# Attention and soft mixture of experts on one core: loads paced from another place in each 256 TensorE instructions, key block 3 asked for sooner, and another order of work in the last stage

## The chip, the cores and the metric

The kernel runs on one core of one Trainium2 chip. The metric is the device time of one execution in microseconds (us). Three runs of the kernel before gave a median of 335.19 us (332.28 to 336.5). The profiled execution is one further run.

## The reference

Attention over 8 batches, 8 heads, 512 local and 32 global tokens of width 64, then a soft mixture of 8 experts with 4 slots each, over the 4,608 tokens of width 512 that the attention gives. All inputs and the output are float32.

```python
s_g  = scale * q_g @ [k_g, k_l]^T              # global queries see every key
s_ll = where(|pos_i - pos_j| <= 32, scale * q_l @ k_l^T, -1e9)
s_l  = [scale * q_l @ k_g^T, s_ll]             # local queries: global keys and a window
out  = softmax(s) @ [v_g, v_l]                 # softmax with + 1e-9 in the denominator
x    = out as (4608, 512)                      # tokens x (heads * 64)
logits = x @ phi                               # 4608 x 32 slots
d = softmax over the tokens;  slot_in = d.T @ x            # 32 x 512
slot_out[e] = relu(slot_in[e] @ w1[e]) @ w2[e]             # 8 experts, 4 slots each
c = softmax over the slots;   return c @ slot_out          # 4608 x 512
```

## The kernel before

The order of the work on every engine is written out by hand: each engine executes its instructions in the order in which the Python code names them, and semaphores hold back one that needs another engine's result.

**Attention** takes 32 steps, one for two heads of one batch (four steps a batch). Step s issues the four copies of values on GpSimd (POOL) that `make_v` makes, the global queries' products on TensorE (PE) when s is even, the scores of step s+1 (`scores`, tile pS), their maximum and shift on VectorE (DVE), the transposes into pT, the values product of step s-1 (128 matmuls in tile pO) and the exponentials on ScalarE (ACT). Once a batch it adds logits and the running slot inputs (`sums`, `add_sums`). A step has some 350 to 460 PE instructions. A float32 matmul is two passes, each a weight load and a matmul, so `mm` counts it as 4.

**Loads.** All transfers are issued by SyncE (SP), from one list, `queue`: "k" is a block of keys and queries for a step (tile kq, 624 KB, 3 buffers), "v" its values (390 KB, 5 buffers), "p" a page of expert weights that stays resident (tile w, 512 KB), "b" a page in a buffer that attention is done with. `counted` adds up the PE instructions. When the count has passed a multiple of 256 by at least 8, it calls `pump`, which issues loads from the list as long as their sum is under BUDGET (with `debt` carried to the next call) and makes each of them wait for the PE instruction at which it was called. `need` issues without such a wait what a step cannot go without: before, `need(kqs, 3)` at the head of step 2 is where key block 3 is issued, behind the list's earlier entries.

**The last stage** follows the last batch's sums. `turn_logits` transposes the logits. `first_product(r, ph)` multiplies the slot inputs of experts 4r to 4r+3 by w1; `denominators` inside it has the DVE wait for a small PE product. `hidden` is relu and scale on the DVE, 8 transposes into pM on PE and two copies on ACT. `weights(g)` is the softmax over slots (DVE, ACT, DVE), `turn_weights(g)` its transpose into pT and a copy on ACT. `second_product(h, m0, m1)` multiplies by the half h of w2's columns, `slot_outputs` brings the sum into tile sa, and `combine(h, b)` multiplies the combine weights of batch b by sa, copies the result out of pS, pT or pM (ACT and DVE in turn) and stores 512 KB (tile ob). Weight pages 47 to 54 (`new_slot`, i from 0) go into the buffers of w1 pages that the first product has read, and so do pages 55 to 63.

Of the kernel before, what the change touches and what calls it, by code (L numbers as in the profile page):

```python
# [7 lines left out]
F32 = mybir.dt.float32  # L8
# [6 lines left out]
B, H, SL, SG, D = 8, 8, 512, 32, 64  # L15
E, SE, DM, FF = 8, 4, 512, 1024
NS = E * SE
P = 128
VD = D + 1
NP = 4 * B  # L20
# [22 lines left out]
NBF = 192 + 512  # L43

NRES = 30


def block_window(c):
# [11 lines left out]
def kernel(ctx, tc, kq, vS, phi, w1, w2, cst, cbf, out):  # L60
# [13 lines left out]
    pS = psum.tile([P, 2, 512], F32, name="pS")  # L74
    pT = psum.tile([P, 2, 512], F32, name="pT")
    pO = psum.tile([P, 2, 512], F32, name="pO")
    pM = psum.tile([P, 2, 512], F32, name="pM")
    pM0, pM1 = pM[:, 0, :], pM[:, 1, :]
# [19 lines left out]
    def bc(ap, n):  # L98
        return ap.unsqueeze(len(ap.shape)).broadcast_to(list(ap.shape) + [n])
# [4 lines left out]


    npe = [0]
    block = [0]

    def counted(n, ins):
        npe[0] += n  # L110
        if npe[0] // 256 > block[0] and npe[0] % 256 >= 8:
            block[0] = npe[0] // 256
            pump(ins)
        return ins

    def mm(o, l, r, start=True, stop=True):
        return counted(2 if l.dtype == BF16 else 4, nc.tensor.matmul(o, l, r, start=start, stop=stop))  # L117

    def tr(o, src, idn):
        return counted(2, nc.tensor.transpose(o, src, idn))  # L120
# [15 lines left out]
    queue, wt = [], {}  # L136
    npage = [0]
# [4 lines left out]
    def page_into(t):  # L142
        k, e, a, f = pages[npage[0]]
        npage[0] += 1
        wt[k, e, a, f] = t
        return nc.sync.dma_start(t, w1[e, a] if k == 0 else w2[e, a, f])
# [9 lines left out]
    def in_slot(i, shape, dtype, name):  # L156
        return slots[i].tile(shape, dtype, tag=f"pg{i}", name=name, bufs=1)
# [5 lines left out]
    def load_borrowed(_):  # L163
        pool, tag = (kqp, "kq") if len(slots) < NRES + 3 else (wp, "w")
        slots.append(None)
        return page_into(pool.tile([P, 1024], F32, tag=tag, name=f"w{npage[0]}"))

    LOAD = {"b": (load_borrowed, 512 * 1024), "k": (load_kq, 128 * KQC * 4), "v": (load_v, 128 * 6 * 2 * VD * 4), "p": (load_res, 512 * 1024)}

    queue = [("k", 0), ("k", 1), ("v", 0), ("k", 2), ("v", 1), ("v", 2), ("p", 0), ("v", 3), ("p", 0), ("v", 4), ("p", 0)]  # L170
    for s in range(3, NP, 2):
        queue += [("k", s)] + ([("k", s + 1)] if s + 1 < NP else []) + [("p", 0)]
        queue += [("v", v) for v in (s, s + 1) if 5 <= v < NP]
        queue += [("p", 0)]
    np_left = NRES - sum(k == "p" for k, _ in queue)
    assert np_left <= 0, np_left
# [5 lines left out]
    def allowed(kind, s):  # L182
        if kind == "k":
            o = s - 3
            return o < 0 or now["a"] >= (o if o % 2 == 0 else o - 1)
        if kind == "v":
            o = s - 5
            return o < 0 or now["c"] >= 2 * (o // 2) + 2
        return now[s[0]] >= s[1] if kind == "b" else True

    BUDGET = 1_150_000
    debt = [0]

    def issue(after=None):
        kind, s = queue.pop(0)
        f, size = LOAD[kind]
        ins = f(s)
        if after is not None:
            tc.add_manual_dep(ins.ins, after.ins.name, mybir.DependencyInfo(
                mybir.DependencyClass.Sync, mybir.DependencyReason.DATA), reason="pace")  # L200
        return size

    def pump(after):
        got = debt[0]
        while queue and allowed(*queue[0]) and got + LOAD[queue[0][0]][1] / 2 < BUDGET:
            got += issue(after)
        debt[0] = max(0, got - BUDGET)

# [394 lines left out]
    two_pages()  # L603


    hTs = {}

    def denominators():
        tot = pT[:, 1, 1:2]
        mm(tot, qmat, wl)  # L610
        nc.vector.tensor_scalar_add(rt, tot, GUARD)
        nc.vector.reciprocal(rt, rt)
        nc.vector.tensor_scalar_mul(rte, con[:, C_EM:C_EM + 2], rt)

    def first_product(r, ph):
        for hc in range(4):
            if hc == 3 and r == 0:
                denominators()
            for n in range(2):
                for j in range(4):  # L620
                    mm(ph[32 * j:32 * j + 32, n, :], sT[hc // 2][:, hc % 2, :],
                       wt[0, 4 * r + j, hc, 0][:, 512 * n:512 * n + 512], hc == 0, hc == 3)

    def hidden(r, ph):
        hs = in_slot(8 + r, [P, 2, 512], F32, f"hs{r}")
        hTs[r] = in_slot(10 + r, [P, 8, P], F32, f"hT{r}")
        for n in range(2):
            nc.vector.tensor_scalar(hs[:, n, :], ph[:, n, :], 0.0, rte[:, r:r + 1], ALU.max, ALU.mult)
        for n in range(2):
            for f in range(4):  # L630
                tr(pM[:, n, P * f:P * f + P], hs[:, n, P * f:P * f + P], ident)
            nc.scalar.copy(hTs[r][:, 4 * n:4 * n + 4, :], pM[:, n, :].rearrange("p (f q) -> p f q", f=4))
# [4 lines left out]
    def turn_logits(g, bank):  # L637
        for k in range(4):
            tr(bank[:, P * k:P * k + P], lT[:, 4 * g + k, 0:P], ident)

    def weights(g, bank):
        n = 16 if g < 2 else 2
        lvs[g] = xp.tile([P, n, NS], F32, tag="xT", name=f"lv{g}", bufs=4) if g < 2 else keep.tile([P, n, NS], F32, name="lvg")
        lv, cm = lvs[g], xp.tile([P, 16], F32, tag="cm", name=f"cm{g}")
        c = cm[:, 0:n]
        if g < 2:
            v = bank.rearrange("p (t s) -> p t s", s=NS)
        else:
            v = lv
            for k in range(2):  # L650
                nc.vector.transpose(lv[:, k, :], lT[:, (4, 7)[k], P:LW])
        nc.vector.reduce_max(c, v, axis=AX.X)
        nc.vector.tensor_tensor(lv, v, bc(c, NS), ALU.subtract)
        nc.scalar.activation(lv, lv, AF.Exp)
        nc.vector.reduce_sum(c, lv, axis=AX.X)
        nc.vector.tensor_scalar_add(c, c, GUARD)
        nc.vector.reciprocal(c, c)
        nc.vector.tensor_tensor(lv, lv, bc(c, NS), ALU.mult)

    def turn_weights(g, bank):  # L660
        lv = lvs[g]
        if g < 2:
            cTs[g] = xp.tile([P, 4, P], F32, tag="xT", name=f"cT{g}", bufs=4)
            for k in range(4):
                tr(bank[:, P * k:P * k + P], lv[:, 4 * k:4 * k + 4, :].rearrange("p t s -> p (t s)"), ident)
            nc.scalar.copy(cTs[g], bank.rearrange("p (k q) -> p k q", k=4))
        else:
            cTs[g] = keep.tile([2 * NS, 1, P], F32, name="cTg")
            tr(bank[0:2 * NS, 0:P], lv.rearrange("p t s -> p (t s)"), ident)
            nc.scalar.copy(cTs[g][:, 0, :], bank[0:2 * NS, 0:P])  # L670

    def second_product(h, m0, m1):
        for m in range(m0, m1):
            r, f = m // 8, m % 8
            for j in range(4):
                mm(pO[32 * j:32 * j + 32, h, 0:256], hTs[r][:, f, 32 * j:32 * j + 32],
                   wt[1, 4 * r + j, h, f // 4][:, 256 * (f % 4):256 * (f % 4) + 256], m == 0, m == 15)
# [3 lines left out]
    def slot_outputs(h):  # L681
        nc.vector.tensor_copy(so[:, h], pO[:, h, 0:256])
        mm(pO[:, h, 0:256], qmat, so[:, h])
        nc.vector.tensor_copy(sa[:, h], pO[:, h, 0:256])
# [6 lines left out]
    def combine(h, b):  # L691
# [11 lines left out]
        else:  # L703
            for gg in range(2):
                nc.sync.dma_start(ov[4 * gg:4 * gg + 4, 0:SG, cs], o[:, gg, :])

    turn_logits(0, pM0)
    turn_logits(1, pM1)
    first_product(0, pO)
    new_slot = lambda i: page_into(in_slot(i, [P, 1024], F32, f"w{npage[0]}"))  # L710
    for i in range(8):
        new_slot(i)
    weights(0, pM0)
    weights(1, pM1)
    weights(2, None)
    turn_weights(0, pT[:, 0, :])
    turn_weights(1, pT[:, 1, :])
    hidden(0, pO)
    turn_weights(2, pT[:, 0, :])
    first_product(1, pS)  # L720
    i = 16
    while npage[0] < len(pages):
        new_slot(i)
        i += 1
    assert i <= 26, i
    second_product(0, 0, 4)
    hidden(1, pS)
    second_product(0, 4, 16)
    so = keep.tile([P, 2, 256], F32, tag="xg0", name="so")
    sa = keep.tile([P, 2, 256], F32, tag="acc", name="sa")  # L730
    slot_outputs(0)
    for b in range(B + 1):
        combine(0, b)
    second_product(1, 0, 16)
    slot_outputs(1)
    for b in range(B + 1):
        combine(1, b)
# [74 lines left out]
```

## Time and profile before

| | |
|---|---|
| median of three runs | 335.19 us (332.28 to 336.5) |
| the profiled execution's own time | 336.67 us |
| its span, first to last instruction | 334.9 us |
| PE / DVE / ACT / POOL busy | 244.9 / 158.0 / 120.9 / 100.8 us |
| moved by DMA | 77.10 MB, mean 230 GB/s |
| mean granted TensorE clock | 0.908 of full speed |

The attention runs from the first scores at 6.5 us to about 241 us, the serial end of the slot softmax to about 257 us, then the expert products and the output to 334.9 us. Busy shares are means over these stages; what ends a stage is read from the waits in it. In the rows, "<-issue" is idle time in which the engine waited for no semaphore that the profile shows. "pO L117 x64" is a group of 64 matmuls made in line 117 (`mm`) with result in pO. Numbers after an instruction in square brackets are its idle time before it and who ended it.

### The profile page before, as it was taken

The numbers are of one execution on the slowest core, as the hardware profiler recorded it, in microseconds if no ns is written. First come the engines' busy times: TensorE is split into PE (matmuls) and PEld (weight loads), VectorE is DVE, ScalarE is ACT, GpSimd is POOL, SyncE is SP. The second block draws the span as 40 slices with busy tenths as digits, with TensorE's granted clock in tenths as the row PEclk, the third lists the DMA queues.
The fourth block names the chain that finished last, engine by engine and source line by source line (L and its number), as shares of the span: only waits on it lengthen the run. The fifth ranks groups of instructions, "written<-read, shape, count | busy, mean of one in ns | idle before, by whom it ended". The sixth has DMA issues, their size and how long they took to land.

```text
span 334.9 us, 15942 instructions
## 1 busy us (share of the span) xinstructions
PE 244.9 (73%) x7345; PEld 166.7 (50%) x7345; DVE 158.0 (47%) x269; ACT 120.9 (36%) x279; POOL 100.8 (30%) x196
## 2 busy tenths in 40 slices
PE   8629568678757978776867877788668739979850
PEld 5417457547535766562756466476433223445420
DVE  0733553728465485573627465674441370133340
ACT  0413443435444355552435345454630021123230
POOL 1630535253363543734243443724400000000000
PEclk9996987979999799996979989999987967999985
DMA  7774776855777773873864596751799852939594
GB/s 239 292 251 159 257 241 222 277 186 156 243 250 230 257 272 115 264 251 131 263 226 141 151 326 203 259 155 42 216 373 396 308 217 106 406 125 338 182 342 139
DMA packets 27907, 77.10 MB, mean 230 GB/s; under 512 B 2368, under 2 KB 11456, under 8 KB 27840
## 3 DMA queue, kind: packets, MB, share of 16 engines
q1 hardware_dynamic: 27840, 76.08, 66.7%
q8 instruction: 57, 0.93, 1.1%
q14 instruction: 10, 0.08, 0.1%
HBM read 67.16 MB, written 8.91 MB: 227 GB/s over the span
## 4 chain that ended last, share of the span: by engine, by line
PE 63%; issue 13%; DVE 11%; ACT 7%; DMA 2%; SPq 1%; DVEq 0%; POOLq 0%; POOL 0%; ACTq 0%
PE pS L117 18%; PE pO L117 17%; PE pM L117 14%; PE pT L120 6%; PE pM L120 6%; DMA kq<-in_kq_dram 2%; ACT w L251 2%; PE pM L446 2%; DVE acc L439 2%; DVE ob L699 1%; DVE x L292 1%; DVE mx L242 1%; DVE w L244 1%; PE pT L117 1%; ACT r L283 1%
## 5 line engine op out<-in xcount | busy, mean ns | idle before, releaser
L242 DVE TENSOR_REDUCE mx<-pS 128x8 f32<-128x1024 f32 x32 | 39.2, 1224 | 74.5 <-PE pS L117 74.2
L117 PE MATMUL pS<-kq 64*32 64x128 f32 x2048 | 43.1, 286 | 11.1 <-issue 11.1
L365 POOL COPY xg<-og 32x64 f32<-32x64 f32 x62 | 14.2, 229 | 107.5 <-ACT og L361 105.6
L117 PE MATMUL pO<-va,w 128*32 128x65 f32 x768 | 41.5, 232 | 4.9 <-issue 4.9
L117 PEld LDWEIGHTS pS<-kq 64*32 64x32 f32 x2048 | 36.9, 110 | 14.1 <-issue 13.3
L117 PE MATMUL pO<-v,w 128*32 128x65 f32 x768 | 40.7, 233 | 3.3 <-issue 3.2
L117 PE MATMUL pO<-vb,w 128*32 128x65 f32 x512 | 39.4, 233 | 4.0 <-issue 3.9
L244 DVE TENSOR_TENSOR w<-pS,mx 128x1024 f32<-128x1024 f32 x32 | 39.2, 1224 | 1.1
L117 PEld LDWEIGHTS pO<-v,w 128*32 128x32 f32 x768 | 33.3, 116 | 7.2 <-issue 4.9
L117 PEld LDWEIGHTS pO<-va,w 128*32 128x32 f32 x768 | 34.0, 117 | 3.2 <-issue 3.2
L117 PEld LDWEIGHTS pO<-vb,w 128*32 128x32 f32 x512 | 31.9, 116 | 6.0 <-issue 6.0
L347 ACT ACTIVATE eg<-pM 128x384 f32<-128x384 f32 (+2 forms) x48 | 14.9, 343 | 54.6 <-PE pM L120 54.6
L117 PE MATMUL pM<-kq 64*32 64x32 f32 (+1 forms) x384 | 23.5, 345 | 14.6 <-DMA kq<-in_kq_dram 5.4
L251 ACT ACTIVATE w<-pT 128x1024 f32<-128x1024 f32 x32 | 32.5, 1015 | 0.6 <-PE pT L120 0.6
L260 POOL COPY va<-v 128x650 f32<-128x650 f32 x32 | 23.2, 724 | 31.1 <-issue 21.5
L117 PEld LDWEIGHTS pM<-kq 64*32 64x32 f32 x384 | 9.2, 113 | 36.1 <-issue 11.0
L120 PE MATMUL pT<-con,w 64*128 64x64 f32 x512 | 24.5, 239 | 0.7 <-ACT w L251 0.7
L292 DVE TENSOR_TENSOR x<-pO,r 128x512 f32<-128x512 f32 x32 | 22.1, 692 | 3.3
L120 PEld LDWEIGHTS pT<-con,w 64*128 64x128 f32 x512 | 19.8, 147 | 7.7 <-issue 5.9
L261 POOL COPY va<-v 32x650 f32<-32x650 f32 x32 | 23.0, 719 | 2.0
L117 PE MATMUL pS<-cb 64*32 64x512 bf16 x256 | 16.5, 412 | 8.3 <-issue 4.7
L309 ACT COPY sgr<-pM 128x480 f32<-128x480 f32 x16 | 8.9, 559 | 34.5 <-PE pM L117 34.4
(146 smaller groups left out, 412.1 us busy)
## 6 DMA issues: line engine op xcount, KB each, us to landing
w<-in_w_dram SPq DMA_DIRECT2D x60, 512.0 KB, 5.1
kq<-in_kq_dram SPq DMA_DIRECT2D x32, 624.0 KB, 5.0
v<-in_vS_dram SPq DMA_DIRECT2D x32, 390.0 KB, 3.5
out_dram<-ob SPq DMA_DIRECT2D x16, 512.0 KB, 6.0
xw<-in_w_dram SPq DMA_DIRECT2D x4, 512.0 KB, 7.6
out_dram<-ob SPq DMA_DIRECT2D x4, 128.0 KB
cb<-in_cbf_dram SPq DMA_DIRECT2D x1, 176.0 KB, 2.4
con<-in_cst_dram SPq DMA_DIRECT2D x1, 130.0 KB, 4.8
```

The lines of the kernel that those rows point to most:

```text
L117: return counted(2 if l.dtype == BF16 else 4, nc.tensor.matmul(o, l, r, start=start, stop=stop))
L120: return counted(2, nc.tensor.transpose(o, src, idn))
L242: nc.vector.reduce_max(mx, g, axis=AX.X)
L244: nc.vector.tensor_tensor(ws[s], g, bc(mx, P), ALU.subtract)
L251: nc.scalar.activation(ws[s], pT.rearrange("p r (u q) -> p (r u q)", q=64), AF.Exp, scale=SCALE)
L260: nc.gpsimd.tensor_copy(va, v[:, 0:5])
L261: nc.gpsimd.tensor_copy(va[0:32], v[0:32, 1:6])
L292: nc.vector.tensor_tensor(xs[b][:, :, P * p:P * p + P].rearrange("p t (h d) -> p h t d", h=2), o[:, :, :, 0:D], bc(r.rearrange("p (h t) -> ...
L309: nc.scalar.copy(at_cols(sgr, FULL, 0, [(32, 3), (P, 5), (1, 32)]), pM0[:, 0:480].rearrange("p (r m j) -> p r m j", r=3, m=5))
L347: nc.scalar.activation(split(eg[0:w, m:m + k, :]), turned(CG + 64 * u, k, w), AF.Exp, scale=SCALE)
L365: copy(xgs[b // 4][32 * (b % 4):32 * (b % 4) + 32, D * hd:D * hd + D], og[32 * j:32 * j + 32, :])
L439: nc.vector.scalar_tensor_tensor(acc[:, c], acc[:, c], st["al", b], src, ALU.mult, ALU.add)
```

## The change

Four edits. `counted` calls `pump` at the counts 209, 465, 721, ... (PHASE), 52 instructions before or 204 after the former places. BUDGET falls from 1.15 to 1.05 million bytes. The list names key blocks 3 and 4 in front of the first weight pages. In the last stage the combine weights of the first half are made before the first product's denominators, `hidden` is cut into `relu` and `turn_hidden`, the first product of experts 4 to 7 is split around the transposes of the first half, the transposes of the other weights move behind it, and the second half of the second product is dealt out in pairs between the batches of `combine(0, b)`.

```diff
+PHASE = 209
-    block = [0]
+    block = [-1]
     def counted(n, ins):
         npe[0] += n
-        if npe[0] // 256 > block[0] and npe[0] % 256 >= 8:
-            block[0] = npe[0] // 256
+        if (npe[0] - PHASE) // 256 > block[0]:
+            block[0] = (npe[0] - PHASE) // 256
             pump(ins)
         return ins
...
-    queue = [("k", 0), ("k", 1), ("v", 0), ("k", 2), ("v", 1), ("v", 2), ("p", 0), ("v", 3), ("p", 0), ("v", 4), ("p", 0)]
-    for s in range(3, NP, 2):
+    queue = [("k", 0), ("k", 1), ("v", 0), ("k", 2), ("v", 1), ("v", 2), ("k", 3), ("v", 3), ("p", 0), ("k", 4), ("p", 0),
+             ("v", 4), ("p", 0)]
+    for s in range(5, NP, 2):
...
-    BUDGET = 1_150_000
+    BUDGET = 1_050_000
...
-    def first_product(r, ph):
-        for hc in range(4):
+    def first_product(r, ph, hc0=0, hc1=4):
+        for hc in range(hc0, hc1):
...
-    def hidden(r, ph):
-        hs = in_slot(8 + r, [P, 2, 512], F32, f"hs{r}")
-        hTs[r] = in_slot(10 + r, [P, 8, P], F32, f"hT{r}")
+    def relu(r, ph):
+        hs = hss[r] = in_slot(8 + r, [P, 2, 512], F32, f"hs{r}")
         for n in range(2):
             nc.vector.tensor_scalar(hs[:, n, :], ph[:, n, :], 0.0, rte[:, r:r + 1], ALU.max, ALU.mult)
+
+    def turn_hidden(r):
+        hs, hTs[r] = hss[r], in_slot(10 + r, [P, 8, P], F32, f"hT{r}")
         for n in range(2):
...
     turn_logits(0, pM0)
     turn_logits(1, pM1)
+    weights(0, pM0)
     first_product(0, pO)
...
     for i in range(8):
         new_slot(i)
-    weights(0, pM0)
+    relu(0, pO)
     weights(1, pM1)
+    turn_weights(0, pT[:, 0, :])
+    first_product(1, pS, 0, 2)
+    turn_hidden(0)
     weights(2, None)
-    turn_weights(0, pT[:, 0, :])
-    turn_weights(1, pT[:, 1, :])
-    hidden(0, pO)
-    turn_weights(2, pT[:, 0, :])
-    first_product(1, pS)
+    first_product(1, pS, 2, 4)
...
-    second_product(0, 0, 4)
-    hidden(1, pS)
-    second_product(0, 4, 16)
+    relu(1, pS)
+    turn_weights(1, pT[:, 1, :])
+    turn_weights(2, pT[:, 0, :])
+    second_product(0, 0, 8)
+    turn_hidden(1)
+    second_product(0, 8, 16)
...
     for b in range(B + 1):
         combine(0, b)
-    second_product(1, 0, 16)
+        if b < B:
+            second_product(1, 2 * b, 2 * b + 2)
```

**SP, the first loads that wait for PE** (kq3 and v2 are the blocks of steps 3 and 2, w0 is the first weight page). Before:

```order
L154 DMA v2_210<-in_vS_dram 128x780
L146 DMA w0_212<-in_w1_dram 128x1024
L154 DMA v3_214<-in_vS_dram 128x780
L146 DMA w1_306<-in_w1_dram 128x1024
L154 DMA v4_308<-in_vS_dram 128x780
L146 DMA w2_391<-in_w1_dram 128x1024
L150 DMA kq3_393<-in_kq_dram 128x1248
L150 DMA kq4_406<-in_kq_dram 128x1248
```

and now:

```order
L156 DMA v2_191<-in_vS_dram 128x780
L152 DMA kq3_289<-in_kq_dram 128x1248
L156 DMA v3_291<-in_vS_dram 128x780
L148 DMA w0_373<-in_w1_dram 128x1024
L152 DMA kq4_375<-in_kq_dram 128x1248
L148 DMA w1_476<-in_w1_dram 128x1024
L156 DMA v4_478<-in_vS_dram 128x780
L148 DMA w2_576<-in_w1_dram 128x1024
L152 DMA kq5_578<-in_kq_dram 128x1248
```

Key block 3 has left three weight pages and two value blocks behind it, and is paced by PE instruction 468 (in step 1) where it stood at the head of step 2, at count 732. Key block 5 comes behind page 2 and is paced by count 1,236 (before: 1,032).

**DVE, from the last sums to the first half's relu** (lv are the combine weights of batches 0 to 3, rt and rte the denominators that wait for PE, hs the relu). Before:

```order
L602 TENSOR_TENSOR wl<-wq,lrun 128x1
L611 TENSOR_SCALAR rt<-pT 128x1
L612 RECIPROCAL rt<-rt 128x1
L613 TENSOR_SCALAR rte<-con,rt 128x2
L652 TENSOR_REDUCE cm_5340<-pM 128x16
L653 TENSOR_TENSOR lv_5339<-pM,cm_5340 128x512
L655 TENSOR_REDUCE cm_5340<-lv_5339 128x16
```

and now:

```order
L605 TENSOR_TENSOR wl<-wq,lrun 128x1
L657 TENSOR_REDUCE cm_5288<-pM 128x16
L658 TENSOR_TENSOR lv_5287<-pM,cm_5288 128x512
L660 TENSOR_REDUCE cm_5288<-lv_5287 128x16
L661 TENSOR_SCALAR cm_5288<-cm_5288 128x16
L662 RECIPROCAL cm_5288<-cm_5288 128x16
L663 TENSOR_TENSOR lv_5287<-lv_5287,cm_5288 128x512
L614 TENSOR_SCALAR rt<-pT 128x1
L615 RECIPROCAL rt<-rt 128x1
L616 TENSOR_SCALAR rte<-con,rt 128x2
L630 TENSOR_SCALAR hs_5348<-pO,rte 128x512 x2
```

The first combine weights have moved in front of the wait on PE (rt), and relu stands right behind the denominators.

**PE, the end of the second product's second half** (w and hT make pO; sa and cT are `combine`; so and con the second `slot_outputs`). Before:

```order
L117 MATMUL pO<-w_5439,hT_5464 32x256
L117 MATMUL pO<-w_5441,hT_5464 32x256
L117 MATMUL pO<-w_5443,hT_5464 32x256
L117 MATMUL pO<-w_5445,hT_5464 32x256
L117 MATMUL pO<-so,con 128x256
```

and now:

```order
L119 MATMUL pO<-w_5432,hT_5482 32x256
L119 MATMUL pO<-w_5434,hT_5482 32x256
L119 MATMUL pO<-w_5436,hT_5482 32x256
L119 MATMUL pM<-sa,cT_5441 128x256 x2
L119 MATMUL pS<-sa,cT_5441 128x256 x2
L119 MATMUL pO<-w_5430,hT_5482 32x256
L119 MATMUL pO<-w_5432,hT_5482 32x256
```

Four banks of two matmuls of `combine` used to follow one another; now 8 of the second product stand between each pair of banks.

## Rows read from the trace of the kernel before

**Rows 1.** The page: busy times, instruction queue (packets, MB, share), chain by engine.

```profile
PE 244.9 (73%) x7345; PEld 166.7 (50%) x7345; DVE 158.0 (47%) x269; ACT 120.9 (36%) x279; POOL 100.8 (30%) x196
...
q8 instruction: 57, 0.93, 1.1%
...
PE 63%; issue 13%; DVE 11%; ACT 7%; DMA 2%; SPq 1%; DVEq 0%; POOLq 0%; POOL 0%; ACTq 0%
```

**Rows 2.** Waits of PE, 33 to 241 us: total, times, longest.

```profile
PE pS L117 <- issue: 15.8, 10, 2.7
PE pO L117 <- issue: 11.1, 9, 2.5
PE pM L120 <- issue: 5.0, 3, 2.3
...
PE pM L117 <- issue: 3.1, 3, 1.6
```

**Rows 3.** Windows: length, engines' busy time, granted PE clock, DMA share, GB/s.

```profile
40.30:72.90 32.60, 24.63 (x836) 18.78 (x830) 17.04 (x27) 13.94 (x32) 14.63 (x28) 0.84 0.70 230
72.90:100.70 27.80, 20.48 (x830) 15.55 (x830) 16.20 (x26) 13.05 (x31) 12.14 (x24) 1.00 0.66 215
...
216.70:241.00 24.30, 19.20 (x758) 14.37 (x758) 13.98 (x24) 12.87 (x31) 10.73 (x22) 1.00 0.41 128
```

**Rows 4.** Timelines of PE and SP around two waits, and a window before the second.

```profile
144.40 0.25 PE L117 MATMUL pO<-v,w 128*32 128x65 f32 x2 [0.55 <-issue]
145.22 1.78 SPq L150 DMA_DIRECT2D kq<-in_kq_dram  x2
153.50 0.22 PE L117 MATMUL pO<-va,w 128*32 128x65 f32 x1 [2.48 <-issue]
...
75.70:78.80 3.10, 3.05 (x164) 2.67 (x161) 2.76 (x4) 2.02 (x5) 0.00 (x0) 1.00 0.02 5
77.93 1.70 SPq L150 DMA_DIRECT2D kq<-in_kq_dram  x2
80.56 0.41 PE L117 MATMUL pS<-kq 64*32 64x128 f32 x4 [1.10 <-issue]
```

**Rows 5.** The start: SP's issues, key block 3 awaited, the clock behind it, landing.

```profile
15.77 0.33 SPq L146 DMA_DIRECT2D w<-in_w_dram  x1
18.19 9.60 SPq L150 DMA_DIRECT2D kq<-in_kq_dram  x2
25.40 1.87 PE L117 MATMUL pM<-kq 64*32 64x480 f32 x14 [5.44 <-DMA kq<-in_kq_dram]
25.40:33.00 7.60, 7.60 (x232) 5.76 (x235) 2.75 (x4) 2.29 (x7) 0.00 (x0) 0.63 0.50 162
kq<-in_kq_dram SPq DMA_DIRECT2D x32, 624.0 KB, 5.0
```

**Rows 6.** The last stage: timelines of PE, DVE and SP, and a window of the output.

```profile
268.84 0.65 PE L120 MATMUL pT<-con,lv 128*128 128x128 f32 x4 [2.86 <-DVE lv L658]
274.26 1.12 PE L120 MATMUL pT<-con,lv 128*128 128x128 f32 x4 [4.77 <-ACT cT L666]
278.41 7.91 PE L117 MATMUL pS<-w,sT 128*32 128x512 f32 x64
289.31 0.66 PE L120 MATMUL pM<-con,hs 128*128 128x128 f32 x4 [0.67 <-ACT hT L632]
295.35 0.42 DVE L682 COPY so<-pO 128x256 f32<-128x256 f32 x1 [7.54 <-PE pO L117]
305.35 7.11 PE L117 MATMUL pO<-w,hT 128*32 128x256 f32 x128
312.54 0.42 DVE L682 COPY so<-pO 128x256 f32<-128x256 f32 x1 [6.64 <-PE pO L117]
315.88 9.04 SPq L702 DMA_DIRECT2D out_dram<-ob  x8
317.00:329.00 12.00, 5.35 (x48) 2.69 (x44) 4.59 (x7) 3.72 (x7) 0.00 (x0) 0.81 1.02 341
```

More of the change, by code (lines that the diff above doesn't have):

```diff
@@ L603 @@
     two_pages()
-    hTs = {}
+    hTs, hss = {}, {}
     def denominators():
@@ L705, in combine @@
                 nc.sync.dma_start(ov[4 * gg:4 * gg + 4, 0:SG, cs], o[:, gg, :])
+    new_slot = lambda i: page_into(in_slot(i, [P, 1024], F32, f"w{npage[0]}"))
     turn_logits(0, pM0)
     turn_logits(1, pM1)
+    weights(0, pM0)
     first_product(0, pO)
-    new_slot = lambda i: page_into(in_slot(i, [P, 1024], F32, f"w{npage[0]}"))
     for i in range(8):
         new_slot(i)
-    weights(0, pM0)
+    relu(0, pO)
     weights(1, pM1)
+    turn_weights(0, pT[:, 0, :])
+    first_product(1, pS, 0, 2)
+    turn_hidden(0)
     weights(2, None)
-    turn_weights(0, pT[:, 0, :])
-    turn_weights(1, pT[:, 1, :])
-    hidden(0, pO)
-    turn_weights(2, pT[:, 0, :])
-    first_product(1, pS)
+    first_product(1, pS, 2, 4)
     i = 16
```

## The prediction, written before the change was run

> **What bounds the kernel now.** I read the chain that ended last first: 63% of the span is PE's own work and 13% is "issue", time in which PE waited for no semaphore [rows 1]. 13% of 334.9 us is 43.5 us, more than any other engine holds but PE itself. The second view is PE's waits in the attention: four groups end on "issue", 15.8 + 11.1 + 5.0 + 3.1 = 35.0 us in 25 waits [rows 2], 1.4 us each. What is awaited there is told by the DMA queues: one of them moves instructions, 57 packets [rows 1]. PE executes 7,345 matmuls and as many weight loads, 14,690 in all, so a packet holds some 258 of PE's instructions: PE's program comes in blocks of about 256 over the DMA engines that also carry the loads, and PE stops where the next block is not there.
>
> How long it stops hangs on what the DMA engines do. Two key blocks issued at 145.22, 0.82 us after a block of instructions had begun at 144.40, are followed by a wait of 2.48 us that ends at 153.50 [rows 4]. Where the DMA engines had been at 0.02 of their capacity from 75.7 to 78.8 us, the wait is still 1.10 us, although two key blocks were issued at 77.93, after the block's start [rows 4]. So a refill has a time of its own, and a burst that was issued before the refill is asked for delays it further; one issued 0.8 us behind it does not seem to. Third, the windows by batch: steps 4 to 31 take 200.7 us from 40.3 to 241.0, in seven batches of which the first, with a granted clock of 0.84, has 32.6 us, the second at full clock 27.8 us, and the last, with 128 instead of some 215 to 245 GB/s, 24.3 us [rows 3]. In the last stage, the waits of PE are on the DVE and on ACT, which do their work in another order than PE needs it: 2.86 us and 4.77 us [rows 6].
>
> **The change, part by part.** The sum is made against the profiled execution's own 336.67 us, which is 1.5 us above the median of the three runs.
>
> *Key block 3 sooner.* Before, SP issues it at 18.19 and PE, which reached it at 25.40 - 5.44 = 19.96, waits 5.44 us [rows 5]. Now it is paced by PE instruction 468. A load paced by instruction 520 was issued at 15.77 [rows 5]; 52 instructions at 27.8 us / 1,660 = 17 ns (a batch of four steps has 1,660) are 0.9 us, so I put it at about 14.9. From issue to landing takes 5.0 us in the median [rows 5]: 19.9, just when PE comes. Saved: 5.3 us. Behind the wait the clock fell to a mean of 0.63 over 7.6 us in which PE was busy throughout [rows 5]; at full clock the same work takes 0.63 x 7.6 = 4.8 us, at most 2.8 us less, and I take 2.3. New cost: key block 5 is paced by count 1,236 behind page 2, while step 4 wants it some 300 instructions, 5 us, later. Landing takes 5.0 us alone, and half a megabyte ahead of it takes 512 KB / 245 GB/s = 2.1 us more at the highest rate of a batch. Between 0 and 2.5 us, I take 1.3. Together -6.3 us (bounds -8 and -3).
>
> *The place of the loads.* A group of loads moves 52 PE instructions ahead or 204 back in the count. Against the blocks of instructions both mean the same: a burst that begins 0.82 us into a block [rows 4] begins about at its start, since 52 instructions take up to 0.9 us. The burst then ends some 0.8 us earlier before the next refill. Bounds: nothing, if the refill does not care, and all 35.0 us of the waits [rows 2]. The waits can't all go: 1.10 us stood with DMA engines empty. I take the nearer bound from the lightest batch, where loads are about half: 24.3 us for its 1,516 instructions [rows 3] is 16.0 ns each; the 11,570 instructions of steps 4 to 31 would take 185.5 us at that pace, 15.2 us under 200.7. The load stays denser than there, so I take 13.5: some 0.4 us from each of 25 waits, 10 us, and 3.5 from the clock, which cost the first batch up to 32.6 - 27.8 = 4.8 us against the second [rows 3].
>
> The Trainium skill says otherwise (Runtime: NRT & Kernel Launch, Instruction fetch mechanics): the sequencer fetches the next 16 KiB, 256 instructions, while the present ones run, so crossing a block is mostly hidden. The size agrees with the packets here; that it is hidden does not, since 25 waits took 35.0 us [rows 2]. By that rule this term would be 0 and the sum 320.
>
> *The smaller BUDGET* and the pages put behind keys cost nothing by themselves: pages come up to 1,228 instructions later, but the last of the "p" pages is still issued at count 11,988, in step 28, and the first product begins after step 32 and the softmax's end. The cover is that stretch; without it a page costs its 512 KB / 341 GB/s = 1.5 us each.
>
> *The last stage, first half.* Today it runs from the end of the first product, 268.84 - 2.86 = 265.98, to the copy of the slot outputs at 295.35: 29.4 us [rows 6]. Now PE does, in a row: transposed weights 0.65; the other first product, in two parts, 7.91; the hidden transposes twice 0.66 + 0.67 + 0.66 = 2.0; the other weights' transposes 0.65 and, behind an ACT copy, about 1.2; the second product 7.11; the hidden transposes again 2.0 [rows 6]. That is 21.5 us, with 0.3 for hand-overs 21.8: -7.6. The DVE work on the first weights, for which PE now waits 2.86, lies beside the first product; relu and the second weights lie beside the first part of the other first product, and the ACT copies, 4.77 us late today, behind them. If that cover failed, these two waits would come back.
>
> *Second half.* From one slot-output copy to the next it takes 312.54 - 295.35 = 17.2 us, 7.11 of them the second product's other half alone on PE [rows 6]. Dealt out between the combines, it hides in the waits for copies, but only as far as PE is idle there. Between 0 and -7.1; PE is busy most of that stretch, so I take the lower middle, -3. *Output.* The stores ran at 341 GB/s [rows 6], 4.45 MB each half, 13.1 us. The first half's would begin 7.6 us sooner, the second's 10.6, so they come 3.0 us closer: 17.1 us between the first stores is now 14.1, still above 13.1, but the small last stores of the first half run into the second. I take 0.6 us for that (0 to 3). Together -10 us (bounds -12 and -5).
>
> Sum: 336.67 - 6.3 - 13.5 - 10 = 306.9. Forecast **306 us**.
>
> **The rivals.** *A, the forecast*, 296 to 313 by its own bounds: 0.62. *B, the place of the loads brings nothing*: the refill shares the DMA engines in turns with any burst, or each gain is eaten by the next block, whose burst now lies closer to it. For it: the transfers of a batch keep the DMA engines busy for 0.66 to 0.74 of the time, and a shorter batch makes that denser. Against it: the 2.48 against the 1.10 us [rows 4]. 336.67 - 6.3 - 10 = 320 us; chance 0.17. The Trainium skill has a rule that would make B right (DMA: Bandwidth & Descriptors, Queues, rings and completion order): an engine goes round between its queues packet by packet, so a refill would wait for one packet, not for a burst. The trace does not look so, since the long waits follow double bursts [rows 4]. *C, the waits go almost wholly and the clock stays up*: 21 of the 35.0 us and 5 more by the clock, with -12 at the end: 336.67 - 6.3 - 26 - 12 = 292; chance 0.13. *D, slower*: the burst now starts so near the refill that it gets ahead of it on the DMA engines. Then each of some 45 blocks in steps 4 to 31 has the long wait instead of the one it has without a burst, 2.48 - 1.10 = 1.4 us more: 336.67 + 45 x 1.4 - 16.3 = 383 us. It decides when the refill is asked for later than the 20 or so instructions, 0.3 us, that lie between a block's first instruction and the paced one. Against it: at 77.93 the burst stood behind the refill and did not hold it [rows 4]. For it: the margin was 0.8 us there and is 0.3 now. Chance 0.04. The rest, 0.04, is a wait that I don't see and that brings it back to about 330.
>
> **How the numbers follow.** 306 is the likeliest case's sum. The range takes in A with its bounds and B with 2 us above it, and the upper part of C: 290 to 322; outside lie half of C's lower part, D and the rest, under 0.2. A difference of 2%, 6.7 us, is about what a measurement of this kernel tells from no change. A, B and C are all faster by more than that: 0.92; the rest is the same, 0.04; D is slower, 0.04.
>
> **What would show it.** In the changed kernel's trace: the wait for key block 3 gone or under 1 us, and one of 0 to 2.5 us for key block 5; PE's waits on "issue" from step 4 to 31 at some 20 to 25 us instead of 35.0, with hardly any above 2 us; batches of 25 to 27 us and fewer windows at half the clock; in the last stage no wait of PE on the DVE's weights, some 22 us from the first product to the first slot-output copy and 14 from that to the second. I am wrong if the "issue" waits stay at 35 us (B), if they grow and follow every burst (D), or if the stores, and not PE, set the end, with the DMA engines full from the first store to the last.

## The result and the profile after

The changed kernel takes 307.21 us in the median of four runs (306.95 to 309.7), the kernel before 335.85 (332.28 to 341.05, four runs beside it): a ratio of 0.920 with a 95% interval of 0.910 to 0.929. The ratio counts only executions within 1.5% of the fastest of their kernel, as do the ratios below. The forecast was 306. The profiled execution took 307.42 us, its span is 305.6. By stages, each from the first instruction of one to that of the next in the two profiled spans:

| stage | before | after | change | forecast |
|---|---|---|---|---|
| start to step 4 | 40.3 | 29.9 | -10.4 | -7.6 |
| steps 4 to 31 | 200.7 | 191.3 | -9.4 | -12.2 |
| softmax's end and first product | 25.0 | 25.3 | +0.3 | 0 |
| first product's end to first slot-output copy | 29.4 | 20.4 | -9.0 | -7.6 |
| to the second slot-output copy | 17.2 | 15.0 | -2.2 | -3 |
| to the end | 22.4 | 23.6 | +1.2 | +0.6 |

The forecast's 1.3 us for key block 5 is set in the second row here, since PE comes to that block in step 4.

The page of the changed kernel: busy times, instruction queue, chain by engine.

```profile
PE 237.3 (78%) x7345; PEld 159.5 (52%) x7345; DVE 158.2 (52%) x269; ACT 121.2 (40%) x279; POOL 101.2 (33%) x196
...
q8 instruction: 57, 0.93, 1.2%
...
PE 68%; issue 10%; DVE 8%; ACT 6%; DMA 4%; SPq 0%; POOLq 0%; POOL 0%; DVEq 0%; ACTq 0%
```

The 57 packets of instructions are the same as in [rows 1]; the chain's "issue" is 10% of 305.6, 31 us, where it was 43.5. PE's waits from step 4 to step 31 of the changed kernel, 29.9 to 221.2 us (total, times, longest), which answer [rows 2]:

```profile
PE pS L119 <- issue: 11.8, 7, 2.5
PE pO L119 <- issue: 8.3, 12, 2.3
...
PE pM L119 <- issue: 2.0, 3, 1.1
PE pM L119 <- DMA kq<-in_kq_dram: 1.9, 2, 1.7
PE pM L122 <- issue: 1.9, 2, 1.2
PE pT L122 <- issue: 1.6, 1, 1.6
```

[rows 2] begin at 33 us, and step 4 only at 40.3: two of their waits, 3.4 us, belong to the start. From 40.3 to 241.0 us the two larger groups of the kernel before, and PE's busy time, are

```profile
PE pS L117 <- issue: 14.8, 9, 2.7
PE pO L117 <- issue: 8.6, 8, 2.5
...
40.30:241.00 200.70, 154.01 (x5792) 115.69 (x5786) 112.72 (x182) 92.00 (x220) 87.39 (x168) 0.93 0.64 211
```

With the other two groups of [rows 2] that makes 31.5 us in 23 waits before, and the issue rows after add up to 25.6 us in 25: two more waits, shorter ones, and new ones for keys. The same seven batches by windows (length, engines' busy time, granted PE clock, DMA share, GB/s), which answer [rows 3]:

```profile
29.90:60.07 30.17, 24.56 (x836) 17.12 (x832) 16.86 (x27) 13.95 (x32) 14.71 (x28) 0.89 0.77 261
60.07:87.46 27.39, 20.56 (x832) 15.47 (x832) 16.31 (x26) 13.06 (x31) 12.12 (x24) 1.00 0.76 245
87.46:112.76 25.30, 20.33 (x832) 15.41 (x833) 16.26 (x26) 12.90 (x31) 12.63 (x25) 1.00 0.73 244
112.76:140.93 28.17, 21.46 (x837) 16.41 (x837) 16.38 (x26) 13.19 (x32) 12.54 (x25) 0.94 0.74 245
140.93:169.58 28.65, 22.81 (x877) 17.33 (x877) 16.66 (x27) 13.13 (x32) 13.36 (x26) 0.94 0.63 216
169.58:196.21 26.63, 20.43 (x832) 15.44 (x833) 16.25 (x26) 12.96 (x31) 11.29 (x22) 1.00 0.74 241
196.21:221.23 25.02, 20.35 (x760) 15.41 (x760) 14.04 (x24) 12.91 (x31) 11.09 (x22) 0.93 0.56 188
```

The batches with a clock of 0.94 or less are the long ones but for the last, which has fewer instructions. The start, which answers [rows 5]: the timeline with SP's issue of key block 3 and of key blocks 5 and 6, and PE's only wait for keys above 1 us.

```profile
14.36 0.33 SPq L152 DMA_DIRECT2D kq<-in_kq_dram  x1
...
26.25 3.90 SPq L152 DMA_DIRECT2D kq<-in_kq_dram  x2
...
32.61 1.86 PE L119 MATMUL pM<-kq 64*32 64x480 f32 x14 [1.72 <-DMA kq<-in_kq_dram]
```

And the window behind PE's coming to key block 3, where the clock used to fall to 0.63:

```profile
17.00:22.00 5.00, 4.98 (x154) 3.12 (x148) 1.79 (x4) 1.85 (x4) 2.68 (x4) 0.86 0.90 308
```

Key block 3 is issued 3.8 us sooner than in [rows 5], and nothing waits for it. The last stage, which answers [rows 6]: PE, then DVE and SP.

```profile
246.47 0.66 PE L122 MATMUL pT<-con,lv 128*128 128x128 f32 x4
247.06 3.64 PE L119 MATMUL pS<-w,sT 128*32 128x512 f32 x32
250.63 0.66 PE L122 MATMUL pM<-con,hs 128*128 128x128 f32 x4
251.96 0.66 PE L122 MATMUL pM<-con,hs 128*128 128x128 f32 x4 [0.68 <-ACT hT L637]
252.55 3.64 PE L119 MATMUL pS<-w,sT 128*32 128x512 f32 x32
256.12 0.66 PE L122 MATMUL pT<-con,lv 128*128 128x128 f32 x4
257.50 0.30 PE L122 MATMUL pT<-con,lvg 128*64 128x128 f32 x1 [0.73 <-ACT cT L671]
...
266.97 0.42 DVE L687 COPY so<-pO 128x256 f32<-128x256 f32 x1 [9.31 <-PE pO L119]
281.96 0.42 DVE L687 COPY so<-pO 128x256 f32<-128x256 f32 x1 [0.21 <-PE pO L119]
...
285.33 9.70 SPq L707 DMA_DIRECT2D out_dram<-ob  x8
295.12 2.58 SPq L710 DMA_DIRECT2D out_dram<-ob  x2
```

The waits of 2.86 and 4.77 us are gone; what is left on PE are hand-overs of 0.7 us. The end of the changed kernel by windows:

```profile
294.00:297.00 3.00, 0.00 (x0) 0.00 (x0) 0.00 (x0) 0.00 (x0) 0.00 (x0) 0.65 1.04 343
...
300.00:303.00 3.00, 0.00 (x0) 0.00 (x0) 0.00 (x0) 0.00 (x0) 0.00 (x0) 0.50 0.24 62
303.00:306.00 3.00, 0.00 (x0) 0.00 (x0) 0.00 (x0) 0.00 (x0) 0.00 (x0) 0.50 0.07 25
```

From 300 us on hardly anything moves: the large stores ran at some 340 GB/s, the last two, small ones drain at 62 and less.

### The profile page after: what moved, and what is told of

It is laid out like the page before. It is cut to its first block, busy times and chain, and to the rows that moved or that the text cites. A ratio compares the mean times of both kernels' runs of the same rounds, so it can differ in the third digit from the quotient of the medians.

```text
span 305.6 us, 15942 instructions
## 1 busy us (share of the span) xinstructions
PE 237.3 (78%) x7345; PEld 159.5 (52%) x7345; DVE 158.2 (52%) x269; ACT 121.2 (40%) x279; POOL 101.2 (33%) x196
## 4 chain that ended last, share of the span: by engine, by line
PE 68%; issue 10%; DVE 8%; ACT 6%; DMA 4%; SPq 0%; POOLq 0%; POOL 0%; DVEq 0%; ACTq 0%
PE pO L119 19%; PE pS L119 18%; PE pM L119 15%; PE pT L122 7%; PE pM L122 6%; DMA kq<-in_kq_dram 4%; DVE acc L442 2%; ACT w L254 2%; PE pM L449 1%; DVE x L295 1%; PE pT L119 1%; DVE ob L704 1%; ACT r L286 1%; DVE mx L245 1%; DVE w L247 1%
## 5 line engine op out<-in xcount | busy, mean ns | idle before, releaser
L119 PE MATMUL pS<-kq 64*32 64x128 f32 x2048 | 41.2, 277 | 12.4 <-issue 12.4
L368 POOL COPY xg<-og 32x64 f32<-32x64 f32 x62 | 14.3, 231 | 98.4 <-ACT og L364 96.4
L119 PEld LDWEIGHTS pS<-kq 64*32 64x32 f32 x2048 | 35.0, 107 | 15.3 <-issue 14.4
L119 PE MATMUL pO<-vb,w 128*32 128x65 f32 x512 | 38.6, 231 | 2.6 <-issue 2.6
L263 POOL COPY va<-v 128x650 f32<-128x650 f32 x32 | 23.2, 726 | 20.0 <-issue 7.9
L122 PE MATMUL pT<-con,w 64*128 64x64 f32 x512 | 23.7, 234 | 2.3 <-issue 1.6
L122 PEld LDWEIGHTS pT<-con,w 64*128 64x128 f32 x512 | 19.1, 143 | 7.2 <-issue 5.5
L265 POOL COPY vb<-v 64x520 f32<-64x520 f32 x32 | 19.8, 619 | 1.9
```

The source lines that it names most:

```text
L263: nc.gpsimd.tensor_copy(va, v[:, 0:5])
L265: nc.gpsimd.tensor_copy(vb[64:128], v[64:128, 0:4])
L368: copy(xgs[b // 4][32 * (b % 4):32 * (b % 4) + 32, D * hd:D * hd + D], og[32 * j:32 * j + 32, :])
```

## The experiments

Times are medians with the range of all runs in brackets. The kernel before has 337.98 us (331.27 to 350.27, 8 runs) beside the new list, the new place, place with BUDGET and the last stage alone; 338.65 (331.04 to 349.06, 7) beside BUDGET alone, the old place and the places 144 and 81; 336.99 (331.52 to 342.87, 11) beside the old BUDGET, the place 233, the loads left out and the stores. The changed kernel was not run again beside them, so what is said against its 307.21 us compares separate sessions. The executions of the kernel before scatter by several per cent, and so do those of most kernels that hold only a part of the change; the changed kernel's lie within 1%. So a single part is read from its stage in the trace beside the median; but the trace, too, is of one execution, and stands for its kernel only where the executions agree.

**One part alone.** Kernel before with the new list:

```diff
-    queue = [..., ("v", 2), ("p", 0), ("v", 3), ("p", 0), ("v", 4), ("p", 0)]
-    for s in range(3, NP, 2):
+    queue = [..., ("v", 2), ("k", 3), ("v", 3), ("p", 0), ("k", 4), ("p", 0), ("v", 4), ("p", 0)]
+    for s in range(5, NP, 2):
```

> The kernel before with the new list of loads alone (key block 3 and 4 sooner); old place, old BUDGET, old last stage. Theory (three separate gains: start, place of the loads, last stage): step 4 begins some 6 to 10 us sooner, steps 4 to 31 take about 200 us as before, so 326 to 330 us. Rival (the list itself is what quietens the attention, since pages come later): steps 4 to 31 fall to some 191 us too, and the time to about 317 us.

334.13 us (328.76 to 339.03), ratio 0.989 (0.970 to 1.008): not told from no change. In its trace (336.81 us) step 4 begins at 32.7 us instead of 40.3, the 7.6 that the start was to bring. But steps 4 to 31 take 206.0 us there, not some 200, with 36.2 us of issue waits: what the start gained is lost behind it, and the span is 335.0 us where it was 334.9.

Kernel before with the new place:

```diff
+PHASE = 209
...
-        if npe[0] // 256 > block[0] and npe[0] % 256 >= 8:
...
+        if (npe[0] - PHASE) // 256 > block[0]:
```

> The kernel before with the new place of the loads alone (count 209 of each 256). Theory: steps 4 to 31 take 188 to 194 us instead of 200.7, PE's waits on issue fall from 35 to some 27 us, the wait for key block 3 stays at 5 us: 324 to 329 us. Rival (the place brings nothing, the refill shares the DMA engines in turns): 335 us, waits of 35 us.

331.64 us (326.77 to 336.35), ratio 0.985 (0.964 to 1.005): not told from no change either. In the trace, which is of the longest of the four runs (336.35 us), step 4 begins at 38.1 us and steps 4 to 31 take 202.7 us, not 188 to 194, with 30.1 us of issue waits, where the theory had 27 and the rival 35, and one of 3.0 us for keys.

Kernel before with the smaller BUDGET:

```diff
-    BUDGET = 1_150_000
+    BUDGET = 1_050_000
```

> The kernel before with the smaller BUDGET alone (1.05 million bytes; old place, list and last stage). After the place alone left steps 4 to 31 at 202.7 us and place with BUDGET gave 189.2. Theory 1 (BUDGET is the whole of it: bursts lie at another place of the steps): steps 4 to 31 at 187 to 193 us, waits on issue some 23 us. Theory 2 (it takes both): steps 4 to 31 at 197 us or more, waits on issue over 30 us.

333.73 us (325.66 to 339.01), inside the scatter of before. The fastest run is the profiled one: there steps 4 to 31 took 189.9 us, as short as in the changed kernel, though its issue waits were 28.5 us, not the 23 of theory 1. So the old place can have a good execution; it does not have one each time.

Place and BUDGET, both edits above:

> The kernel before with the new place and the smaller BUDGET, old list and last stage. Theory: BUDGET by itself is worth little, so within 3 us of the kernel with the new place alone. Rival (smaller bursts are what lets the refill through): at least 5 us below it.

327.53 us (321.67 to 332.69), ratio 0.970 (0.948 to 0.992): some gain, not yet 2% for certain. The 4.1 us below the place alone lie between the theory's 3 and the rival's 5, inside the scatter of both. In the trace steps 4 to 31 take 189.2 us with 23.2 us of issue waits.

Kernel before with the new last stage only:

```diff
-    hidden(0, pO)
...
+    relu(0, pO)
...
+    turn_hidden(0)
...
+        if b < B:
+            second_product(1, 2 * b, 2 * b + 2)
```

> The kernel before with the new order of the last stage alone. Theory: the last stage is 10 us shorter and nothing else moves: 325 to 327 us. Rival (part of the gain at the end came from pages and clock that the quicker attention leaves behind): less than 6 us, 330 us or more.

324.92 us (318.15 to 329.26). The three pieces of the last stage are 20.4, 15.0 and 24.0 us, as in the changed kernel (20.4, 15.0, 23.6): this part needs none of the others.

**One part undone.** The changed kernel with the old place:

```diff
-        if (npe[0] - PHASE) // 256 > block[0]:
+        if npe[0] // 256 > block[0] and npe[0] % 256 >= 8:
```

> The changed kernel with the old place (multiples of 256, plus 8); new list, BUDGET and last stage. Theory 1 (the place is worth nothing by itself): steps 4 to 31 at 189 to 194 us as in the changed kernel, 305 to 310 us. Theory 2 (it takes both): 198 us or more, 314 us or more.

325.78 us (322.32 to 326.21): 18.6 above the changed kernel, with ranges far apart. PE's waits in steps 4 to 31 with the old place back:

```profile
PE pS L119 <- issue: 13.6, 10, 2.8
PE pO L119 <- issue: 13.3, 9, 3.8
...
PE pM L122 <- issue: 4.1, 2, 2.3
PE pM L119 <- issue: 3.2, 3, 2.0
```

The window of these steps:

```profile
31.80:236.90 205.10, 153.91 (x5789) 115.07 (x5788) 112.42 (x182) 92.20 (x220) 87.43 (x168) 0.93 0.65 218
```

34.2 us of issue waits in 24 at a clock of 0.93. The same steps of the changed kernel, with 25.6 us of them and 0.96:

```profile
29.90:221.20 191.30, 150.49 (x5791) 112.58 (x5786) 112.76 (x182) 92.11 (x220) 87.73 (x168) 0.96 0.71 235
```

Of the 13.8 us between 205.1 and 191.3, 8.6 are issue waits and 3.4 the clock, by PE's busy time for the same matmuls (153.91 and 150.49).

The changed kernel with the old BUDGET:

```diff
-    BUDGET = 1_050_000
+    BUDGET = 1_150_000
```

> The changed kernel with BUDGET at 1,150,000 again, the place at 209 and all else kept. Theory 1 (place and BUDGET work only together, as the old place with the new BUDGET cost 18 us): 318-326 us, issue waits of TensorE above 29 us. Theory 2 (the BUDGET brings nothing of its own once the place is 209, as the prediction had it): 305-310 us.

314.36 us (307.49 to 315.92). The fastest of the four runs is as fast as the changed kernel, the others took 6 to 9 us longer, so neither theory is shown. In the fastest, which was profiled, steps 4 to 31 take 191.0 us with 30.6 us of issue waits.

**The place moved.** The changed kernel with PHASE at 233, 144 and 81 in place of 209:

```diff
-PHASE = 209
+PHASE = 233
```

> The changed kernel with the loads 24 TensorE instructions further on in each 256 (233 instead of 209). Theory 1 (the loads only have to start once the refill, which begins with a block, is through, and end before the next one): 233 lies between 209 and the old place, 264 = 8 of the next block, which gave 325.8, so 308-320 us with issue waits of 27-33. Theory 2 (209 is not special, everything behind the refill's end is as good): 305-309 us.

315.61 us (308.43 to 322.9). The shortest of the four is near the changed kernel and the longest near the old place, so 233 is not told from 209; its executions lie 14 us apart, where those at 209 lie within 3. In the profiled one (317.23 us) steps 4 to 31 take 196.8 us with 29.0 us of issue waits.

```diff
-PHASE = 209
+PHASE = 144
```

> The changed kernel with PHASE 144: every burst is issued some 40 instructions ahead of a block's first, so its packets stand in front of that block's refill. Theory (a refill waits for every packet issued before it): each of the 45 refills waits out its own block's burst, 3 to 5 us, steps 4 to 31 take 250 us or more. Rival (turns): 189 to 200 us.

338.31 us (336.72 to 339.89, two runs), 31 above the changed kernel. PE's waits in steps 4 to 31 with the place at 144:

```profile
PE pS L119 <- issue: 18.0, 7, 3.9
PE pO L119 <- issue: 15.6, 10, 3.3
PE pM L122 <- issue: 5.4, 2, 3.1
...
PE pT L122 <- issue: 3.5, 1, 3.5
```

The window of these steps:

```profile
33.70:249.90 216.20, 160.84 (x5791) 120.13 (x5786) 112.53 (x182) 92.41 (x220) 87.56 (x168) 0.88 0.59 203
```

With a last group of 0.6 these are 43.1 us in 21 waits, 2.1 us each where the changed kernel has 1.0, and the clock stands at 0.88. The steps take 216.2 us, between the 250 of the theory and the 200 of the rival. Asking for the loads 65 instructions sooner costs more than all four edits gain.

```diff
-PHASE = 209
+PHASE = 81
```

> The changed kernel with PHASE 81: every burst begins half a block of instructions later, some 150 instructions after the block's first. Theory (a refill waits for what is left of the burst before it): the burst's end comes some 2 us later against the next refill, steps 4 to 31 grow from 191 to 200 to 215 us, waits on issue to 35 us or more. Rival (the refill shares the engines in turns, the place does not matter): 189 to 195 us.

339.96 us (338.54 to 341.37, two runs): 43.4 us of issue waits in 27, clock 0.90, 218.4 us for steps 4 to 31, above the 200 to 215 of the theory. So, by place: 209 gives 307, 233 gives 308 to 323, the old place (264, which is 8 of the next 256) 326, and 81 and 144, behind that, 340 and 338.

**The loads left out.** The changed kernel computes on the first key and value blocks again and again, so that the transfers of 29 key blocks and 27 value blocks, and their part of the result, are left out; the weight pages stay.

```diff
     def load_kq(s):
+        if s >= 3:
+            kqs[s] = kqs[s % 3]
+            return None
...
     def load_v(s):
+        if s >= 5:
+            vs[s] = vs[s % 5]
+            return None
```

> The changed kernel without the key blocks from 3 on and the value blocks from 5 on: those steps compute on the first blocks again, so that part of the result is left out; the weight pages still come at the same places. Theory 1 (a refill of TensorE's instructions is held up by the load bursts that are still draining): of the 26.7 us of issue waits of TensorE in 30:240 at most 13 are left, and none over 1.5 us except behind pages; the stretch of steps 4 to 31 falls from 191 to 175-182 us, the whole to 288-298. Theory 2 (the waits belong to TensorE's own sequencer, whatever the transfers do): over 20 us of waits are left and the time stays at 303-309.

287.05 us (286.14 to 287.95, two runs). PE's waits in steps 4 to 31 without the loads:

```profile
PE pO L119 <- issue: 6.2, 10, 0.9
PE pS L119 <- issue: 6.2, 7, 1.1
...
PE pM L122 <- issue: 1.9, 2, 1.2
PE pT L122 <- issue: 1.2, 2, 0.7
...
PE pM L119 <- issue: 0.8, 1, 0.8
```

The window of these steps:

```profile
29.00:201.20 172.20, 141.94 (x5794) 107.67 (x5786) 112.27 (x182) 92.02 (x220) 87.34 (x169) 1.00 0.29 99
```

PE executes the same instructions, and its waits on "issue" are 16.3 us in 22, none over 1.2, with the clock at its upper level, 2.4 GHz (1.00), all the way. So 9.3 of the changed kernel's 25.6 us are the transfers' doing, and 16.3, some 0.7 us per wait, are there anyway: more than the 13 that the expectation allowed, though the steps (172.2 us) and the whole (287.05) came out just below its ranges.

The traces also date the packets of the instruction queue, 16,384 bytes each, 46 of them in steps 4 to 31. In the kernel before and in the changed one every issue wait of these steps ends 1.2 to 1.6 us after such a packet has landed: these waits are refills. The eight longest before begin within 0.5 us of the start of their packet, and in the microsecond ahead of it the DMA engines were at 0.82 to 1.03 of their capacity; without the loads they were at 0.05 in the mean. Sorted by length, us and times in steps 4 to 31:

| kernel | issue waits | of 1.8 us or more | shorter |
|---|---|---|---|
| before | 31.5, 23 | 18.1, 8 | 13.5, 15 |
| changed (209) | 25.6, 25 | 8.9, 4 | 16.7, 21 |
| changed, old place | 34.2, 24 | 17.4, 7 | 16.7, 17 |
| changed, 144 | 43.1, 21 | 35.0, 12 | 8.0, 9 |
| changed, 81 | 43.4, 27 | 29.2, 11 | 14.3, 16 |
| changed, loads left out | 16.3, 22 | none | 16.3, 22 |

The place sets how many refills come late behind busy DMA engines; most of the short waits are there without any loads.

**The last stores.** The changed kernel with the small stores (b = 8) behind batch 2 in both halves:

```diff
-    for b in range(B + 1):
+    for b in (0, 1, 2, B, 3, 4, 5, 6, 7):
         combine(1, b)
```

> The changed kernel with combine 8 of each half (the small stores of 128 KB) moved behind combine 2, so that the last store is a large one of 512 KB. Theory 1 (the last 4.5 us, at 62 GB/s and less, are the small stores draining alone): the end comes 2 to 4 us sooner, 303-305 us, and so copy to end is 20-22 us instead of 23.6. Theory 2 (the last 4 us are the landing of whatever store is last): same as the changed kernel, 306.5-308.

305.81 us (303.15 to 309.5, six runs), ratio to before 0.911 (0.904 to 0.918). Its end, by windows:

```profile
291.00:294.00 3.00, 1.79 (x16) 0.84 (x16) 2.06 (x3) 1.17 (x2) 0.00 (x0) 1.00 0.64 142
...
300.00:303.00 3.00, 0.00 (x0) 0.00 (x0) 0.00 (x0) 0.00 (x0) 0.00 (x0) 0.50 0.64 219
```

From the second slot-output copy to the end it takes 21.1 us, 2.5 less than the changed kernel. The slow drain is no longer alone at the end; part of it now shows as the 142 GB/s at 291. In the median 1.4 us are left of it, which the runs do not separate from none, as the ranges overlap. It is the fastest complete version that was run.

## Why the prediction held, and where its terms were off

**Key block 3.** The mechanism was right: 5.44 us of waiting became none, and key block 5 took 1.72 where 1.3 was put. The term was mis-sized: the stage gave 10.4, not 7.6. The clock's part held (at 17 to 22 us after, of 5 us at 0.86, 0.7 are lost, where 0.63 over 7.6 had cost 2.8). What the prediction did not count is "issue" at the start: in the stretch from 17 to 42 us PE's issue waits fell from 4.3 us in three to 1.7 in two. Two of the three, 3.4 us, the prediction had counted with the attention, in [rows 2]. The new list alone gave 7.6, so the rest belongs to the place or to the scatter, of which the start has some: the kernel with the last stage alone began step 4 1.5 us sooner than before, with nothing changed there.

**The place of the loads.** This was the largest term, and the one with the widest bounds. Against the kernel before, issue waits in steps 4 to 31 fell by 5.9 us, where 10 were forecast; PE's busy time for the same matmuls fell by 3.5 (154.01 to 150.49), just what was put on the clock; the steps are 9.4 us shorter, not 12.2. Against the same kernel with the old place the steps are 13.8 us shorter, close to the 13.5. Both can't be the effect of the place alone: the old place with the other three edits had 205.1 us where before had 200.7. With the old place and the new list the traces have 206.0 and 205.1 us, with the old list 200.7, 199.6 and 189.9: the list may cost there what it gains at the start, but single executions scatter as much. So the place is shown to be worth 18.6 us with the other edits in; by itself, on the kernel before, it is not told from nothing, and how the edits work together stays open. That loads hold up the refill of PE's instructions is shown by the kernel without them (9.3 us fewer waits, the clock up from 0.96 to 1.00, 19.1 us less in these steps), by the places 81 and 144, at which the waits were 43.4 and 43.1 us, and by the dates of the packets.

The step that failed in size was the argument for 0.4 us from each of 25 waits, "the burst then ends some 0.8 us earlier before the next refill". The waits did not each get shorter: of the eight long ones four went, 9.2 us, and the shorter ones grew by 3.2. Taken further the argument would make 144 better still, since the burst would end sooner yet; at 144 the time was 31 us longer. That is rival D, a burst that gets ahead of the refill, at 338 instead of 383 us: 21 waits of 2.1 us, not 45 that are each 1.4 us longer. Where between 144 and 209 it sets in was not tried; that 209 lies on its good side, by 0.3 us in the prediction's estimate, was in part luck.

The row on which the 1.4 us rest was read across another wait. Between the key blocks issued at 145.22 and the wait that ends at 153.50 [rows 4] stand

```profile
148.12 0.93 PE L117 MATMUL pS<-kq 64*32 64x128 f32 x48 [1.49 <-issue]
149.46 0.38 SPq L154 DMA_DIRECT2D v<-in_vS_dram  x1
```

so the key blocks are followed by a wait of 1.49 us, not far from the 1.10 behind idle DMA engines, and the 2.48 by the loads issued behind it. That long waits stand behind busy DMA engines is nevertheless so, by the dates of the packets above. The range of the likeliest case, 296 to 313, can't be added up from the bounds of its terms. Of the signs that were named, the issue waits are at 25.6 us (20 to 25), three of them are above 2 us (hardly any), and the batches take 25.0 to 30.2 us (25 to 27).

Rival B fell for this kernel: with the old place it was at 325.8, not at 307. The rule that stood behind it (the Trainium skill, DMA: Bandwidth & Descriptors, Queues, rings and completion order), that an engine serves its queues packet by packet in turn, would have the place matter little; these runs differ by 33 us in the place alone and don't agree. The other rule (the Trainium skill, Runtime: NRT & Kernel Launch, Instruction fetch mechanics), that the fetch is mostly hidden, is nearer without the loads, but 22 waits with 16.3 us are still seen there. Rival C, in which 21 of 35.0 us of waits go and the clock stays up, is near what the kernel without loads does at 287; with all loads no place that was tried comes near it.

**The smaller BUDGET** was costed at nothing. By itself it can't be told from nothing; undone in the changed kernel it left the fastest run at 307.49. Whether it does anything stays open.

**The last stage** came out at -10.0 of a forecast -10, and with the same three pieces in the kernel that changes nothing else. First half: 20.4 us, where adding up PE's work gave 21.8; the product of experts 4 to 7 took 2 x 3.64 = 7.28 instead of 7.91. The cover held: the DVE finished the first weights beside the first product, and no wait on them is left. Second half: 15.0 us against 14.1; the combines and the second product share PE, which is busy throughout (12.50 of the 12.50 us from 270.5 to 283.0). Output: +1.2 instead of +0.6, with the last two small stores draining alone.

So the sum, off by 0.3 us, is better than its terms: 2.8 too little at the start and 2.8 too much in the attention cancel.

## What to carry to other kernels

Where PE's program is long and loads are paced by PE's own progress, "issue" waits on PE are worth a look beside the transfers: where in each 256 instructions a burst starts moved this kernel by 10%, and of five places tried only one kept all its runs below 310 us, so it is tried at several, not argued to one. Sort such waits by length and look at what the DMA engines did ahead of each long one. In a serial stage, write down PE's work in order and put each DVE or ACT result one PE item ahead of its use; the sum of PE's durations forecast this one to within 1.5 us. Look at what drains last: behind the large stores two small ones took the last 5.6 us.

## What the runs showed of the hardware that was not expected

The clock cost PE time beside the waits: for the same matmuls PE was busy for 141.9 us at a mean granted clock of 1.00, 150.5 at 0.96, 153.9 at 0.93 and 160.8 at 0.88, in kernels that had 16.3, 25.6, 34.2 and 43.1 us of issue waits in steps 4 to 31, the last two with single waits of up to 3.9 us. It does not go by the sum of the waits: the profiled run with the old BUDGET had 30.6 us of them at 0.97 and took the same 191.0 us. Steps 4 to 31 of the kernel before hold seven stretches at the lower level, 1.2 GHz (0.50), and each begins 0.3 to 1.5 us behind the end of a single issue wait of 1.9 to 2.7 us; two further waits of 2.3 us have none behind them. Without the loads, with no issue wait over 1.2 us, there is no such stretch in these steps. One of the seven:

```profile
170.30 0.22 PE L117 MATMUL pO<-v,w 128*32 128x65 f32 x1 [2.38 <-issue]
171.00:174.30 3.30, 2.92 (x73) 2.29 (x66) 0.90 (x2) 1.47 (x3) 2.67 (x4) 0.50 0.63 204
```

The two stores of 128 KB behind the second half's 4 MB of large ones move at 62 and then 25 GB/s in the last 5.6 us, with the DMA engines at 0.24 and 0.07 of their capacity, where stores of 512 KB run at some 340. Whether that is their size or their shape no run here tells.
